# Transposes of 64 tokens on the two halves of the array, for groups 17 to 23 of an attention and mixture-of-depths kernel

## The chip, the cores and the metric

One core of one Trainium2 chip. The metric is the device time of one execution in microseconds (us), the median of several executions. Engines are named as in the profile: PE is TensorE's matrix multiply and PEld its weight load, DVE is VectorE, ACT is ScalarE, POOL is GpSimd, SP is SyncE, which only issues DMAs here.

## What is computed

The reference runs a linear attention with decay over blocks of 64 tokens (4 sequences, 8 heads, 768 tokens, 64 channels per head), and feeds its output to a mixture of depths: the 128 tokens of each sequence with the highest gate score go through two matrix products with a ReLU between them and are added back.

```
for b in range(nb):
    intra = (qb @ kb.T * Dmask) @ vb
    inter = (qb * lam_pow) @ kv_state
    out[:, :, sl] = intra + inter
    kv_state = lam_block * kv_state + (kb * rev_pow).T @ vb
...
scores = x @ w_gate
top_idx = argpartition(-scores[b], capacity)[:capacity]
ye = relu(x[b, top_idx] @ w1) @ w2
out[b, top_idx] = x[b, top_idx] + sigmoid(scores[b, top_idx])[:, None] * ye
```

All data is float32.

## The kernel before

The work goes in 24 groups of 128 tokens, six for each of the four sequences. A group's q, k and v lie in three tiles `qn`, `kn`, `vn` of 128 partitions (tokens) by 8 heads by 64 channels, loaded by SP some groups ahead. The order of the work is written out by hand: the last loop of the kernel goes over the groups, and each engine runs its instructions in that order. Groups 0 to 9 are "wide" and treat 128 tokens as one block; from group 10 on each group is two blocks of 64 tokens, and the array is used in quarters of 64 rows by 64 columns.

One iteration g of the loop (called round g) does, from group 10 on, in this order:

- `transposes(g + 1, ...)` (lines 217 to 232): four PE transposes of 128 by 128 for q (two heads each), four for k (L226), and after each four one ACT copy of 128 partitions by 512 out of PSUM (L230), to the tiles `qT` and `kT`.
- every sixth round (16 and 22 here) the gate of an expert step: four transposes of the fetched rows `xs` (L628) and an ACT copy to `xsT` (L633).
- `from_states(g)`: 16 products into the accumulator `o` (L381); `queries_decayed(g + 1)` on POOL, which multiplies `qT` to `qs` (L265); `state_products(g + 1)` into `su` (L327).
- one to three pieces of an expert's two matrix products (`hidden`, L657, with an ACT ReLU at L661; `back`, L669), between them a row of scores (L493) and sums over tables (L541) for the choice of tokens, which DVE does.
- `from_scores(g)`, 16 products into `o` (L403); `scores(g + 1)` into `su` (L285); `outputs(g)`: three ACT copies from `o` to the output tile `x_b`, one of 128 partitions (L433), two of 64 (L435), each between the halves of the partitions; `masked(g + 1)` on DVE, which makes `p` from `su` (L301).
- after a sequence's tokens have been chosen, `fetch` on POOL (L615) reads the chosen rows by an indirect DMA.

PSUM has two tiles `su` and `o` of two banks each and four banks handed out in turn by `bank()` (lines 186 to 195). A transposed group takes two of the four, and so do the row of scores, the sums and each expert product in turn one; whoever gets a bank again waits until the copy that reads it is done.

A matrix product of float32 shows as two records in the trace, a transpose as one. A form such as 64*128 behind a tile is the part of the array that is used: rows by columns.

Of the kernel before, what the change touches and what calls it, by code (L numbers as in the profile page):

```python
# [8 lines left out]
FP32 = mybir.dt.float32  # L9
# [8 lines left out]
def kernel(  # L18
# [12 lines left out]
    nc = tc.nc  # L31
# [5 lines left out]
    L = 128  # L37
    C = 64
    NT = S // L
    NHP = H // 2  # L40
# [3 lines left out]
    NG = B * NT  # L44
# [4 lines left out]
    W1 = (8, 8, 9, 10)  # L49
    W2 = (11, 11, 12, 13)  # L50
    WIDE = 10
    KEPT = {11: ((6, 2),), 12: ((8, 2), (10, 2))}
    KEPT.update((g + 4, ((g, 1),)) for g in range(12, 16))
    TINY = 2.0 ** -125
# [4 lines left out]
    att = ctx.enter_context(tc.tile_pool(name="att", bufs=3))  # L59
# [5 lines left out]
    half = [slice(0, C), slice(C, 2 * C)]  # L65
    loaded = {}
# [46 lines left out]
    ident = const.tile([128, 128], FP32, name="ident")  # L113
# [14 lines left out]
    for hp in range(NHP):  # L128
        for hh in range(2):
            h = 2 * hp + hh  # L130
            nc.vector.tensor_tensor_scan(
                out=mask_w[:, hh, hp, :], data0=lam_b[:, h : h + 1].broadcast_to([128, L]),
# [53 lines left out]
    def bank(hold=False):  # L186
        t = next(t for t in free if not any(t is x for x in held))
        free[:] = [x for x in free if x is not t] + [t]
        if hold:
            held.append(t)  # L190
        return t

    qTs, qss, kTs, kds, ps_ = {}, {}, {}, {}, {}
# [8 lines left out]
    def wide(g):  # L202
        return g < WIDE

    def keys_decayed(g):
        if g >= NG:
            return
        kd = att.tile([128, H, D], FP32, name="kd", bufs=2)
        pw = kpow_w if wide(g) else kpow
        nc.gpsimd.tensor_tensor(  # L210
            out=kd[:], in0=loaded[g][0][:],
            in1=pw[:].rearrange("p a b -> p (a b)").unsqueeze(2).broadcast_to([128, H, D]),
            op=ALU.mult,
        )
        kds[g] = kd

    def transposes(g, name):
        if g >= NG:
            return
        if wide(g - 1):  # L220
            tp = tq if name == "qT" else tk
        else:
            tp = bank()
        t = loaded[g][1 if name == "qT" else 0]
        for hp in range(NHP):
            nc.tensor.transpose(  # L226
                tp[:, hp * L : (hp + 1) * L], in_=t[:, 2 * hp : 2 * hp + 2, :], identity=ident[:]
            )
        dst = att.tile([128, NHP, L], FP32, name=name)
        nc.scalar.copy(out=dst[:].rearrange("p a i -> p (a i)"), in_=tp[:])  # L230
        (qTs if name == "qT" else kTs)[g] = dst

    def first_scores():
        got = []
# [201 lines left out]

    kept = {g + i for v in KEPT.values() for g, n in v for i in range(n)}

# [325 lines left out]
    def loads_to(n):  # L764
        while next_load[0] < min(n, NG):
            load(next_load[0])
            next_load[0] += 1

    def ends(g):
        return g >= 0 and g % NT == NT - 1  # L770

    def find(b):
        for i in range(NGR):
            hits(b, i)
# [6 lines left out]
    def shares(g):  # L781
        at = (g - WIDE) % NT
        if g + 1 == NG:
            return (0, 0, 1)
        few = at < 2 if g < WIDE + NT else at >= 4
        return (1, 0, 1) if few else (1, 1, 1)
# [57 lines left out]
    for g in range(-1, NG):  # L844
        loads_to(g + 4)
        for rows in KEPT.get(g, ()):
            rows_out(*rows)
        for do in weights.get(g, []):
            do()
        if wide(g):  # L850
            if g < 0:
                keys_decayed(0)
            wide_step(g)
            if g == 0:
                constants()
            if g == 1:
                narrow_constants()
        else:
            transposes(g + 1, "qT")
            transposes(g + 1, "kT")  # L860
            if NGR and ends(g - 5):
                for i in range(NGR):
                    gate, more = expert((g - 5) // NT, i)
                    if i == 0:
                        gate()
                    else:
                        pieces.append(gate)
                    pieces.extend(more)
            if g + 1 == NG:
                products(1)  # L870
            from_states(g)
            settle(g)
            queries_decayed(g + 1)
            state_products(g + 1)
            next_state(2 * g + 2)
            decay_state(2 * g + 3)
            keys_decayed(g + 2)
            share = shares(g)
            products(share[0])
            if NGR:  # L880
                column_sums(g - 2)
                row(g - 1)
            products(share[1])
            second(g + 1)
            if ends(g - 3):
                take((g - 3) // NT)
            if NGR:
                compare(g - 1)
                if ends(g - 2):
                    find((g - 2) // NT)  # L890
            products(share[2])
            from_scores(g)
            scores(g + 1)
            outputs(g)
            store(g)
            masked(g + 1)
            gate_scores(g)
            flush()
# [54 lines left out]
```

## Time and profile before

| | |
|---|---|
| median of 3 executions | 176.22 us (176.14 to 176.54) |
| the profiled execution's own time | 176.97 us |
| its span in the profile | 175.2 us |
| busy share of PE, PEld, DVE, ACT, POOL | 93%, 76%, 57%, 38%, 49% |
| granted TensorE clock, mean | 0.995 of full speed |

Times in the rows below are us from the start of the span. A row of the timeline gives the start, the time to the end of the last of its instructions, the engine, the line, what is written and read, and how many instructions were merged. A busy PE is one that has matmuls in flight, whose ends are modelled; the pace is read from starts. "idle before" in square brackets is the engine's idle time and what ended it.

### The profile page before, as it was taken

How to read it: one execution, taken by the hardware profiler on the slowest of the kernel's cores; microseconds unless marked ns; L12 is line 12 of the kernel's file. 1: busy time of each engine (PE TensorE's matmuls, PEld its weight loads, DVE VectorE, ACT ScalarE, POOL GpSimd, SP SyncE). 2: the span in 40 equal slices, each digit the busy share in tenths (PEclk: the TensorE clock that was granted, in tenths of full speed). 3: DMA queues.
4: the chain of work that ended last, by engine and by line, in shares of the span. 5: the costliest groups of instructions: out<-in, count | busy, mean ns of one | idle time of the engine just before them, and what ended most of it. 6: DMA issues, size and time to landing. Idle time of an engine off the chain costs nothing.

```text
span 175.2 us, 7559 instructions
## 1 busy us (share of the span) xinstructions
PE 162.9 (93%) x3250; PEld 132.4 (76%) x3250; DVE 99.9 (57%) x351; ACT 66.4 (38%) x170; POOL 86.1 (49%) x101
## 2 busy tenths in 40 slices
PE   6999999997999999998859999999999999999990
PEld 2778988886989898985444899975866999459970
DVE  3956567777766666567434545866656757530011
ACT  0552744443333456254031644542553545012100
POOL 2258966155489718745259264658468500202022
PEclk9999999999999999999999999999999999999998
DMA  4999999999999899999889997999893322011000
GB/s 108 227 219 225 236 209 237 232 237 223 208 239 269 188 253 223 283 277 308 239 200 229 200 259 177 228 191 244 190 191 112 123 62 62 8 55 60 0 30 30
DMA packets 92210, 31.94 MB, mean 182 GB/s; under 512 B 75793, under 2 KB 90129, under 8 KB 92178
## 3 DMA queue, kind: packets, MB, share of 16 engines
q1 hardware_dynamic: 91376, 29.37, 73.3%
q0 software_dynamic: 656, 2.10, 3.9%
q8 instruction: 25, 0.41, 1.0%
q14 instruction: 7, 0.06, 0.1%
q10 hardware_dynamic: 146, 0.01, 0.0%
HBM read 24.12 MB, written 7.34 MB: 180 GB/s over the span
## 4 chain that ended last, share of the span: by engine, by line
PE 59%; DMA 18%; SPq 8%; DVE 5%; issue 3%; ACT 2%; POOL 2%; POOLq 1%; ACTq 0%; DVEq 0%
DMA qn<-in_q_dram 11%; PE m L657 10%; PE m L226 9%; PE m L669 9%; DMA kn<-in_k_dram 6%; PE o L396 4%; PE su L279 4%; PE o L381 3%; PE su L327 3%; PE o L403 3%; PE su L285 3%; SPq L76 3%; PE o L370 3%; PE m L318 2%; PE m L696 2%
## 5 line engine op out<-in xcount | busy, mean ns | idle before, releaser
L657 PE MATMUL m<-xsT,w_sb 128*128 128x128 f32 x256 | 33.1, 280 | 0.0
L657 PEld LDWEIGHTS m<-xsT,w_sb 128*128 128x128 f32 x256 | 30.3, 192 | 1.4 <-ACT xsT L633 0.6
L265 POOL TENSOR_TENSOR qs<-qT,qpow 128x512 f32<-128x512 f32 x14 | 18.3, 1308 | 20.3 <-ACT qT L230 20.3
L669 PE MATMUL m<-w_sb,hs 128*128 128x512 f32 x48 | 24.0, 611 | 0.3 <-DMA w_sb<-in_moe_w_dram 0.3
L210 POOL TENSOR_TENSOR kd<-kn,kpow 128x512 f32<-128x512 f32 x14 | 15.1, 1078 | 6.3 <-DMA kn<-in_k_dram 6.3
L661 ACT ACTIVATE hs<-m 128x128 f32<-128x128 f32 x32 | 8.9, 277 | 24.0 <-PE m L657 19.1
L340 POOL TENSOR_TENSOR decayed<-state,decay 128x256 f32<-128x256 f32 x23 | 16.7, 726 | 2.2 <-DVE state L359 1.8
L226 PE MATMUL m<-ident,qn 128*128 128x128 f32 x92 | 14.7, 282 | 2.9 <-DMA qn<-in_q_dram 2.9
L263 POOL TENSOR_TENSOR qs<-qT,qpow 128x512 f32<-128x512 f32 x8 | 10.2, 1272 | 14.8 <-ACT qT L230 14.7
L301 DVE TENSOR_TENSOR p<-su,mask 128x512 f32<-128x512 f32 x14 | 9.7, 690 | 12.0 <-PE su L285 10.3
L230 ACT COPY qT<-m 128x512 f32<-128x512 f32 x23 | 13.4, 584 | 6.8 <-PE m L226 5.0
L295 DVE TENSOR_TENSOR p<-su,mask_w 128x1024 f32<-128x1024 f32 x10 | 12.2, 1220 | 6.5 <-PE su L279 6.5
L359 DVE TENSOR_TENSOR state<-su,decayed 128x256 f32<-128x256 f32 x23 | 9.8, 424 | 10.1 <-POOL decayed L340 5.7
L427 ACT COPY x_b<-o 128x512 f32<-128x512 f32 x10 | 5.9, 586 | 22.9 <-PE o L396 20.3
L226 PE MATMUL m<-ident,kn 128*128 128x128 f32 x92 | 13.8, 273 | 0.0
L230 ACT COPY kT<-m 128x512 f32<-128x512 f32 x23 | 13.6, 592 | 0.1
L226 PEld LDWEIGHTS m<-ident,qn 128*128 128x128 f32 x92 | 9.9, 141 | 4.8 <-DMA qn<-in_q_dram 3.5
L210 POOL TENSOR_TENSOR kd<-kn,kpow_w 128x512 f32<-128x512 f32 x10 | 10.4, 1045 | 4.9 <-DVE kpow_w L136 4.9
L403 PEld LDWEIGHTS o<-vn,p 64*64 64x64 f32 x448 | 7.8, 134 | 6.2 <-issue 1.5
L506 DVE TENSOR_SCALAR_CACHE_REDUCE table<-sc_row,sc 128x128 bf16<-128x128 f32 (+4 forms) x20 | 12.1, 604 | 0.0
L669 PEld LDWEIGHTS m<-w_sb,hs 128*128 128x128 f32 x48 | 8.0, 192 | 4.9 <-issue 4.1
L327 PE MATMUL su<-vn,kd 64*64 64x64 f32 x400 | 10.3, 221 | 1.4 <-issue 0.7
(103 smaller groups left out, 295.1 us busy)
## 6 DMA issues: line engine op xcount, KB each, us to landing
vn<-in_v_dram SPq DMA_DIRECT2D x24, 256.0 KB, 5.7
kn<-in_k_dram SPq DMA_DIRECT2D x23, 256.0 KB, 5.0
qn<-in_q_dram SPq DMA_DIRECT2D x23, 256.0 KB, 6.2
out_dram<-x_b SPq DMA_DIRECT2D x18, 256.0 KB, 4.6
w_sb<-in_moe_w_dram SPq DMA_DIRECT2D x16, 256.0 KB
out_dram<-x_b SPq DMA_DIRECT2D x3, 512.0 KB
kn<-in_k_dram SPq DMA_DIRECT2D x2, 128.0 KB
qn<-in_q_dram SPq DMA_DIRECT2D x2, 128.0 KB, 3.4
```

The source lines that it names most:

```text
L210: nc.gpsimd.tensor_tensor(out=kd[:], in0=loaded[g][0][:], in1=pw[:].rearrange("p a b -> p (a b)").unsqueeze(2).broadcast_to([128, H, D]), ...
L226: nc.tensor.transpose(tp[:, hp * L : (hp + 1) * L], in_=t[:, 2 * hp : 2 * hp + 2, :], identity=ident[:])
L230: nc.scalar.copy(out=dst[:].rearrange("p a i -> p (a i)"), in_=tp[:])
L263: nc.gpsimd.tensor_tensor(out=qs[:], in0=qTs[g][:], in1=qpow[:], op=ALU.mult)
L265: nc.gpsimd.tensor_tensor(out=qs[:].rearrange("p a (c i) -> p a c i", c=2), in0=qTs[g][:].rearrange("p a (c i) -> p a c i", c=2), in1=qpow ...
L295: nc.vector.tensor_tensor(out=p[:], in0=su[:], in1=mask_w[:].rearrange("p a b i -> p a (b i)"), op=ALU.mult,)
L327: nc.tensor.matmul(su[half[hh], c, NHP * C + hp * D : NHP * C + (hp + 1) * D], lhsT=kd[half[c], h, :], rhs=vn[half[c], h, :], start=True, ...
L340: nc.gpsimd.tensor_tensor(out=t[:], in0=states[n][:], in1=(decay_w if wide(g) else decay)[:], op=ALU.mult)
L403: nc.tensor.matmul(o_[half[hh ^ c], hh, hp * D : (hp + 1) * D], lhsT=p[half[c], hh, hp * C : (hp + 1) * C], rhs=vn[half[c], 2 * hp + hh, : ...
L506: nc.vector.tensor_scalar(out=table[:, : t * L], in0=rows_[b][:, : t * L], scalar1=scs[b][:, t : t + 1], scalar2=0.0, op0=ALU.is_ge, op1=A ...
L657: nc.tensor.matmul(ph, lhsT=w1_sb[:, dc, f * 128 : (f + 1) * 128], rhs=keep["xsT"][:, dc, :], start=(dc == 0), stop=(dc == NDC - 1),)
L669: nc.tensor.matmul(py[:], lhsT=keep["hs"][:, f, :], rhs=w2_sb[:, :, f, :], start=(f == 0), stop=(f == NFC - 1),)
```

## The change

For groups 17 to 23 (`SIDE = 17`, so in rounds 16 to 22) the eight transposes of 128 tokens are replaced by sixteen of 64 tokens. Tokens 0 to 63 lie in the upper half of the rows of the array and go to one PSUM bank, tokens 64 to 127 in the lower half and go to another; upper and lower alternate. A bank then holds one half of the tokens for q and, behind it, for k. The two ACT copies of 512 columns become four of 256, each of which writes four pieces of 64 columns with a stride. All sixteen transposes stand ahead of the four copies. Groups 0 to 16 keep the old form.

```diff
+    SIDE = 17
...
+    def side_by_side(g):
+        if g >= NG:
+            return
+        to = [bank(), bank()]
+        for i in range(2):
+            t = loaded[g][1 - i]
+            for hp in range(NHP):
+                for c in range(2):
+                    at = (i * NHP + hp) * C
+                    nc.tensor.transpose(
+                        to[c][:, at : at + C], in_=t[half[c], 2 * hp : 2 * hp + 2, :],
+                        identity=ident[half[c], half[c]],
+                    )
+        for i, (name, have) in enumerate((("qT", qTs), ("kT", kTs))):
+            dst = att.tile([128, NHP, L], FP32, name=name)
+            for c in range(2):
+                nc.scalar.copy(
+                    out=dst[:, :, half[c]],
+                    in_=to[c][:, i * NHP * C : (i + 1) * NHP * C].rearrange(
+                        "p (a i) -> p a i", i=C
+                    ),
+                )
+            have[g] = dst
...
-            transposes(g + 1, "qT")
-            transposes(g + 1, "kT")
+            if g + 1 >= SIDE:
+                side_by_side(g + 1)
+            else:
+                transposes(g + 1, "qT")
+                transposes(g + 1, "kT")
```

How the order on the engines moves, at three places. Behind `waits` stand the engines or DMA queues whose semaphores an instruction waits for; in the changed kernel the lines of the old functions are 27 higher (L381 is L408, L327 is L354, L493 is L520, L657 is L684, L633 is L660, L661 is L688). The first place is PE in round 18. Before:

```order
L226 MATMUL m_139<-ident,qn 128x128 [waits DMAHW7_49]
L226 MATMUL m_139<-ident,qn 128x128 x3
L226 MATMUL m_138<-ident,kn 128x128 [waits DMAHW6_49,DVE_49]
L226 MATMUL m_138<-ident,kn 128x128 x3
L381 MATMUL o<-state,qs 64x64 [waits Activation_49,Pool_49]
L381 MATMUL o<-state,qs 64x64 x7
L327 MATMUL su<-vn,kd 64x64 [waits DMAHW0_49,DVE_49,Pool_49]
```

Now, from the eight transposes of k on (the eight of q ahead of them look the same):

```order
L245 MATMUL m_139<-ident,kn 128x64 [waits DMAHW6_49]
L245 MATMUL m_138<-ident,kn 128x64
L245 MATMUL m_139<-ident,kn 128x64
L245 MATMUL m_138<-ident,kn 128x64
L245 MATMUL m_139<-ident,kn 128x64
L245 MATMUL m_138<-ident,kn 128x64
L245 MATMUL m_139<-ident,kn 128x64
L245 MATMUL m_138<-ident,kn 128x64
L408 MATMUL o<-state,qs 64x64 [waits Activation_49,Pool_49]
L408 MATMUL o<-state,qs 64x64 x7
L354 MATMUL su<-vn,kd 64x64 [waits DMAHW0_49,DVE_49,Pool_49]
```

The transposes have doubled in number and take turns between two banks; what follows, and what it waits for, is the same. L381's wait on Activation is for the last of the three output copies of the round before, L435.

The second place is ACT in round 16, whose expert gate stands behind the transposes. Before:

```order
L230 COPY qT_1869<-m0_138 128x512 [waits PE_49,Pool_49]
L230 COPY kT_1875<-m2_140 128x512 [waits DVE_49,PE_49,Activation_49]
L633 COPY xsT_1881<-m3_141 128x512 [waits PE_49]
L661 ACTIVATE hs_1883<-m1_139 128x128 [waits DVE_49,PE_49]
L497 COPY sc_row_1553<-m2_140 128x128 [waits PE_49]
```

Now:

```order
L252 COPY qT_1881<-m0_138 128x4x64 [waits PE_49,Pool_49]
L252 COPY qT_1881<-m2_140 128x4x64 [waits DVE_49,PE_49]
L252 COPY kT_1884<-m0_138 128x4x64 [waits Activation_49]
L252 COPY kT_1884<-m2_140 128x4x64
L660 COPY xsT_1891<-m3_141 128x512 [waits PE_49]
L688 ACTIVATE hs_1893<-m1_139 128x128 [waits DVE_49,PE_49]
```

The copy to `xsT`, which the first expert product reads, now has four copies ahead of it instead of two, and the first bank is read to the end by the third copy, the second by the fourth.

The third place is PE in round 17, where the row of scores and an expert product take the banks of the transposes again. Before:

```order
L541 MATMUL m1_139<-ones_146,table_1931 128x1
L493 MATMUL m0_138<-ident_99,sc_1472 128x128 [waits DVE_49,Activation_49]
L657 MATMUL m2_140<-xsT_1881,w1_sb_97 128x128 [waits Activation_49]
L657 MATMUL m2_140<-xsT_1881,w1_sb_97 128x128 x3
L657 MATMUL m3_141<-xsT_1881,w1_sb_97 128x128 [waits Activation_49]
```

Now:

```order
L568 MATMUL m1_139<-ones_146,table_1941 128x1
L520 MATMUL m0_138<-ident_99,sc_1472 128x128 [waits DVE_49,Activation_49]
L684 MATMUL m2_140<-xsT_1891,w1_sb_97 128x128 [waits Activation_49]
L684 MATMUL m2_140<-xsT_1891,w1_sb_97 128x128 x3
L684 MATMUL m3_141<-xsT_1891,w1_sb_97 128x128 [waits Activation_49]
```

The order is the same, but L493's bank was free after the copy of qT and is now free after the third copy, and the bank of the L657 behind it was free after the copy of kT and is now free after the fourth.

## Rows read from the trace of the kernel before

**Rows 1.** The page: busy time by engine, and shares of the chain that ended last.

```profile
PE 162.9 (93%) x3250; PEld 132.4 (76%) x3250; DVE 99.9 (57%) x351; ACT 66.4 (38%) x170; POOL 86.1 (49%) x101
...
PE 59%; DMA 18%; SPq 8%; DVE 5%; issue 3%; ACT 2%; POOL 2%; POOLq 1%; ACTq 0%; DVEq 0%
```

**Rows 2.** The chain that ended last, in order of time: start, duration, what.

```profile
83.83 6.77 DMA qn<-in_q_dram
...
90.64 1.09 PE m L226 x8
...
111.08 1.02 PE m L226 x8
...
141.80 0.69 DVE p L301
```

**Rows 3.** Timeline of PE and ACT in round 18.

```profile
109.92 0.69 PE L403 MATMUL o<-vn,p 64*64 64x64 f32 x32
...
110.44 0.65 PE L285 MATMUL su<-qT,kT 64*64 64x64 f32 x32
...
110.68 0.37 ACT L433 COPY x_b<-o 128x256 f32<-128x256 f32 x1 [0.38 <-PE o L403]
...
111.02 0.66 PE L226 MATMUL m<-ident,qn 128*128 128x128 f32 x4
111.07 0.74 ACT L435 COPY x_b<-o 64x256 f32<-64x256 f32 x2
...
111.51 0.60 PE L226 MATMUL m<-ident,kn 128*128 128x128 f32 x4
111.84 0.58 ACT L230 COPY qT<-m 128x512 f32<-128x512 f32 x1
...
112.04 0.51 PE L381 MATMUL o<-state,qs 64*64 64x64 f32 x10
...
112.32 0.59 ACT L230 COPY kT<-m 128x512 f32<-128x512 f32 x1
```

**Rows 4.** Timeline of PE in a wide round: products on the two halves.

```profile
24.37 1.16 PE L279 MATMUL su<-qT,kT 64*128 64x128 f32 x16
25.46 1.15 PE L396 MATMUL o<-vn,p 128*64 128x64 f32 x32
```

**Rows 5.** Timeline of PE in rounds 16 and 17: expert products behind the transposes.

```profile
100.39 1.16 PE L657 MATMUL m<-xsT,w_sb 128*128 128x128 f32 x8
...
107.73 0.30 PE L493 MATMUL m<-ident,sc 128*128 128x128 f32 x1
107.94 0.49 PE L657 MATMUL m<-xsT,w_sb 128*128 128x128 f32 x2
```

**Rows 6.** Timeline of ACT in rounds 16 and 17.

```profile
98.66 0.59 ACT L230 COPY qT<-m 128x512 f32<-128x512 f32 x1
99.14 0.59 ACT L230 COPY kT<-m 128x512 f32<-128x512 f32 x1
99.62 0.60 ACT L633 COPY xsT<-m 128x512 f32<-128x512 f32 x1
...
106.83 0.57 ACT L230 COPY qT<-m 128x512 f32<-128x512 f32 x1
107.30 0.59 ACT L230 COPY kT<-m 128x512 f32<-128x512 f32 x1
```

**Rows 7.** Timeline of POOL, DVE and PE in rounds 20 and 21.

```profile
125.03 1.27 POOL L265 TENSOR_TENSOR qs<-qT,qpow 128x512 f32<-128x512 f32 x1 [2.50 <-ACT qT L230]
...
128.94 1.00 POOL L615 DMA_INDIRECT xs<-out_dram,tok  x1 [0.16 <-issue]
...
130.35 0.69 DVE L301 TENSOR_TENSOR p<-su,mask 128x512 f32<-128x512 f32 x1 [1.70 <-PE m L226]
...
131.15 0.69 PE L327 MATMUL su<-vn,kd 64*64 64x64 f32 x32 [0.33 <-issue]
```

**Rows 8.** Timeline of ACT at the start, two windows: copies of 128 x 256.

```profile
6.27 0.70 ACT L245 COPY first<-m 128x256 f32<-128x256 f32 x2
...
6.27 0.97 ACT L245 COPY first<-m 128x256 f32<-128x256 f32 x3
```

## The prediction

> **What bounds the kernel now.** I read the page first: TensorE (PE) is busy 93% of the span, and PE work is 59% of the chain that ended last [rows 1]. That share is an average, so I read the chain in order of time. There the last wait for a load ends at 90.64 us; from then on the chain is PE work alone, eight transposes of 1.02 us in each round among them, until 141.80, where VectorE (DVE) takes over [rows 2]. The seven rounds that the change touches (call the iteration g of the main loop "round g"; it transposes group g + 1, so rounds 16 to 22) lie in that stretch. So PE time taken out would count in full, if nothing else is waiting right behind it. That has to be read round by round from the timeline.
>
> Round 18 shows it [rows 3]. The transposes start at 111.02 and the next PE work, L381, at 112.04. But L381 accumulates into tile o, and o is still being read: the three output copies of ScalarE (ACT, L433 and L435) start at 110.68, after L403, and end at 111.07 + 0.74 = 111.81. The order of the program says that L381 waits for the last of them (Activation among its waits). So PE has only 111.81 to 112.04 = 0.23 us less a hand-over to gain there, however fast the transposes become. What I see: two paths of nearly equal length from L403 to L381, one of them on ACT and untouched by the change.
>
> **The transposes themselves.** Eight records with 128 columns moved become sixteen with 64 columns, alternating between the halves of the array. Nearest rows: L279 uses the same halves (64*128), loads 128 columns per record and moves 128: 16 records from 24.37 to 25.46, 1.09 us, 68 ns each, two at a time [rows 4]. L285 moves 64 columns with four quarters of the array at a time: 32 records from 110.44 to 111.02, 0.58 us, 18 ns each, so about 73 ns per quarter [rows 3]; two at a time that is 36 ns, or 0.58 us for sixteen. Bounds 0.58 and 1.09 us against 1.02 now. I take 0.58, because the columns moved set the pace in both rows and here they are 64. Sixteen loads instead of eight are hidden behind the other half's records, as they are in L279; if that cover is gone, see the slow rival.
>
> The Trainium skill (TensorE: Matmul & The Clock Gate, section LDWEIGHTS) says that a load's time goes by its columns, not by its rows: P/1.2 ns, and that 32 x 128 takes as long as 128 x 128. By it sixteen loads in a row would take 1.71 us (an estimate) and the halves would lose. L279's 68 ns per record with the same 128 columns shows that loads of two halves do overlap or are quicker, so I give that little chance.
>
> **What the saved 0.44 us buys in each round.**
> - Rounds 18 and 19: L381 starts when the output copies have ended plus a hand-over. In round 17 PE starts hidden product L657 at 107.94, 0.05 us after the copy of kT out of the same bank ended (107.30 + 0.59 = 107.89) [rows 5, 6]; L381 has two waits, so I take 0.10. Gain 0.23 - 0.10 = 0.13 each; ends 0 and 0.18. Everything behind L381 is PE work in order, so it is kept. Sum -0.26.
> - Round 20 would gain the same, but gives it to round 21. There the fetch of the expert rows starts on GpSimd (POOL) at 128.94; p (L301) on DVE, though its scores were done before, starts only at 130.35, and L327, which writes the same tile, at 131.15 [rows 7]. POOL works without a gap from qs at 125.03 to that fetch, and qs waits for the two new halves of qT. So what counts for rounds 20 and 21 is when qT is complete: see ACT.
>
> **ACT: two copies of 512 columns become four of 256.** One of 512 takes 0.58 to 0.59 us and starts 0.48 after the one before (98.66, 99.14, 99.62) [rows 6]; one of 256 takes 0.37 (L433) [rows 3]. How close behind each other can the short ones start? Two ends: the output copies do not overlap at all (110.68, 111.07, then 0.74 for two: 0.37 to 0.39 apart) [rows 3]; the copies of 256 columns at the very start do: two end at 6.97, three at 7.24, 0.27 apart [rows 8]. I take 0.27: like the new ones and like qT to kT, those run over all 128 partitions from partition 0, while the output copies shift between the halves of the partitions. Four copies then take 1.06 to the next start instead of 0.96.
> - Round 16: ACT starts qT at 98.66, xsT would start at 99.72 instead of 99.62 and end at 100.33; L657 needs it, at 100.38 with the hand-over, and it starts at 100.39 now [rows 5, 6]. PE comes there 0.44 early and waits: 0.0. The same in round 22, which has the same expert gate: 0.0.
> - Round 17: ACT is held by the gate's exponential until 106.83, whatever PE does. The fourth copy ends at 106.83 + 3 x 0.27 + 0.37 = 108.01; the hidden product writes the same bank and starts at 108.06 instead of 107.94 [rows 5, 6]: +0.11. The 0.13 at L381 is lost in that wait.
> - Rounds 20 and 21: qT is complete 0.27 + 0.37 = 0.64 after its start instead of 0.59: +0.05.
>
> DMA: nothing is issued more or less, no queue is passed. POOL, DVE: no instruction changes.
>
> **Sum.** 0.0 + 0.11 - 0.13 - 0.13 + 0.05 + 0.0 = -0.10 us. The profiled execution took 176.97 us (span 175.2 and 1.77 around it), 0.75 above the median of 176.22; I carry the difference over to the median: 176.1. A measurement of this kernel can tell about 0.2%, 0.35 us, from no change, so this is no change.
>
> **Rivals.**
> - The ACT copies do not overlap (0.375 apart, as the output copies). Round 16: xsT starts at 98.66 + 1.50, L657 at 100.82: +0.42; round 22 the same; round 17: 108.38, +0.44; rounds 18 and 19 -0.26; rounds 20 and 21 +0.16. Sum +1.18: 177.4, slower. If only copies into the same tile fail to overlap, +0.7: 176.9. It decides from about 0.30 us between copies on. For it: the new copies write strided rows of 4 x 64, as L433 does. Against: rows 8 and the overlap of qT and kT. Chance 0.25.
> - The halves do not run side by side as fast. At L279's 1.09 us the copies, which wait for all sixteen records, start 0.49 late: rounds 16 and 22 +0.47 each, 17 +0.11, 18 and 19 +0.07 each, 20 and 21 +0.54: +1.7, 178.0; chance 0.07. If each half record cost as much as a whole one now (16 x 0.128 = 2.04 us), every round would lose 1.0 and rounds 16, 20 and 22 1.4: +7, 183.5; chance 0.04. L279 speaks against that.
> - ACT is better still: copies 0.21 apart, the pure difference of 0.58 and 0.37 for 256 columns. Then xsT comes 0.2 earlier in rounds 16 and 22, round 17 gains 0.05, rounds 18 and 19 up to 0.18 each: -0.8, 175.4, faster. Rows 8 show no pair so close, but there PE's transposes may have held it. Chance 0.15.
>
> **Numbers.** Forecast 0.49. It spreads by the hand-over (rounds 18 and 19: 0 to -0.36 in all) over 175.9 to 176.4; a tenth of it may pass 0.35 on the fast side. Faster: 0.15 + 0.05 = 0.20. Slower: 0.25 + 0.11 = 0.36, of which a little may stay within: 0.35. Same: 0.45. The range takes in the copies without overlap and the fast ACT: 175.4 to 177.6; outside lie the slow halves (0.11) and a tail.
>
> **What would show it.** Right: sixteen records in about 0.6 us; L381 0.1 us after the last output copy with PE idle 0.3 before it; copies of 256 columns 0.27 apart; L657 waiting for xsT in rounds 16 and 22. Wrong: copies 0.37 apart; 1 us or more for the sixteen records; or L381 starting before the output copies end.

## The result and the profile after

The changed kernel takes 178.04 us (median of 12 executions, 176.75 to 180.70) where the kernel before took 175.87 beside it: a ratio of 1.0122, 95% interval 1.0080 to 1.0164. That is 2.2 us slower, not the same. Timed twice more (e2 and e9 below), it came to 1.0017 (0.9977 to 1.0057) and 1.0144 (1.0067 to 1.0222); two of the three intervals lie above 1, so the sign is fairly safe, the size is not.

The profiled execution took 177.48 us, span 175.7. The page: busy time of PE, the queue that carries an engine's instructions (queue, packets, MB, share of the DMA engines), and the shares of the last chain, to be laid beside [rows 1].

```profile
PE 160.3 (91%) x3306; PEld 130.0 (74%) x3306; DVE 100.4 (57%) x351; ACT 67.1 (38%) x184; POOL 85.8 (49%) x101
...
q8 instruction: 26, 0.43, 1.0%
...
PE 40%; POOL 14%; DMA 13%; issue 11%; SPq 7%; DVE 7%; ACT 5%; POOLq 1%; DVEq 0%; ACTq 0%
```

PE is busy 2.6 us less than before and the kernel is longer: "issue", time in which an engine waits for nothing that the profile shows, has gone from 3% to 11% of the chain. That share has to be read by place. Of its 20 us some 15 lie ahead of 46 us, where both kernels do the same work, and e2, the same kernel, has 3%. In the seven changed rounds the two longest pieces of it are these:

```profile
128.87 0.53 issue
...
134.28 0.60 issue
```

Groups of PE work by line, with the idle time ahead of them and what ended it, first in the kernel before, then after:

```profile
L381 PE MATMUL o<-state,qs 64*64 64x64 f32 x416 | 10.0, 224 | 0.2 <-issue 0.2
L285 PE MATMUL su<-qT,kT 64*64 64x64 f32 x448 | 9.1, 218 | 0.2 <-DVE state L359 0.2
```

```profile
L312 PE MATMUL su<-qT,kT 64*64 64x64 f32 x448 | 10.1, 219 | 1.6 <-issue 1.4 <-DVE state L386 0.2
L408 PE MATMUL o<-state,qs 64*64 64x64 f32 x416 | 9.9, 225 | 0.9 <-ACT x_b L462 0.9
```

L408's new 0.9 us is the wait for the output copies that the prediction described. L312's 1.4 us is not in the prediction at all. The steps that it did describe came as described. PE and ACT in round 16:

```profile
97.63 0.46 PE L245 MATMUL m<-ident,qn 64*128 64x64 f32 x8
...
98.27 0.65 PE L655 MATMUL m<-ident,xs 128*128 128x128 f32 x4
...
100.19 0.49 PE L684 MATMUL m<-xsT,w_sb 128*128 128x128 f32 x2 [0.18 <-ACT xsT L660]
```

```profile
98.45 0.65 ACT L252 COPY qT<-m 128x256 f32<-128x256 f32 x2
98.98 0.67 ACT L252 COPY kT<-m 128x256 f32<-128x256 f32 x2
99.51 0.63 ACT L660 COPY xsT<-m 128x512 f32<-128x512 f32 x1
```

The sixteen records take 97.63 to 98.27 = 0.64 us, and a pair of copies starts 0.53 after the pair before, 0.27 a copy. Round 18, beside [rows 3]:

```profile
110.94 0.47 PE L245 MATMUL m<-ident,qn 64*128 64x64 f32 x8
110.99 0.74 ACT L462 COPY x_b<-o 64x256 f32<-64x256 f32 x2
...
111.88 0.51 PE L408 MATMUL o<-state,qs 64*64 64x64 f32 x10 [0.23 <-ACT x_b L462]
```

The copies end at 110.99 + 0.74 = 111.73 and L408 follows 0.15 later. The stretches from one round's transposes to the next one's, the last to the end, show where the time went:

| round | 16 | 17 | 18 | 19 | 20 | 21 | 22 to the end | sum |
|---|---|---|---|---|---|---|---|---|
| before, us | 6.71 | 6.47 | 6.27 | 6.25 | 5.47 | 5.94 | 40.23 | 77.34 |
| after, us | 6.72 | 6.59 | 6.21 | 6.18 | 6.32 | 5.84 | 40.20 | 78.06 |

From round 16 on the kernel is 0.72 us longer, and round 20 alone 0.85. PE there and in round 21:

```profile
128.22 0.65 PE L312 MATMUL su<-qT,kT 64*64 64x64 f32 x29
129.39 0.33 PE L312 MATMUL su<-qT,kT 64*64 64x64 f32 x3 [0.53 <-issue]
...
133.99 0.30 PE L312 MATMUL su<-qT,kT 64*64 64x64 f32 x6
134.89 0.68 PE L312 MATMUL su<-qT,kT 64*64 64x64 f32 x26 [0.60 <-issue]
```

PE stops in the middle of the scores, after 29 of 32 records and after 6 of 32, for 0.74 and 0.82 us from one start to the next, with no tile to wait for. Before, the same scores run through in both rounds:

```profile
128.43 0.65 PE L285 MATMUL su<-qT,kT 64*64 64x64 f32 x32
...
134.37 0.65 PE L285 MATMUL su<-qT,kT 64*64 64x64 f32 x32
```

Round 21 is not longer than before only because L327 waits for a late p there [rows 7], which it does not after.

**The theory.** I counted PE's instructions in the program, a product and its weight load as one each: 6582 before, 6687 after, sixteen more in each of the seven changed rounds (and seven separate waits fewer). The two gaps stand after instruction 5570 and after instruction 5826, exactly 256 apart. The packets of q8 are 16 KB each, 25 before and 26 after, which is one per 256 instructions. The packet that belongs to the first gap starts at 127.03 and PE goes on 2.36 us later; for the second it is 132.60 and 2.29 us. So: PE's instructions come in stretches of 256, one packet each, and where PE works off a stretch before the next one has come, it stands. Halved transposes give it more instructions in less time. Against this stand waits on tiles, and plain scatter between executions. In what follows a boundary is the place between two stretches, and a stretch is entered when its first product starts.

The Trainium skill (Runtime: NRT & Kernel Launch, section Instruction fetch mechanics) says that an engine's sequencer fetches its program in blocks of 256 instructions by a DMA queue of its own while it runs the block before, and that crossing such a boundary is mostly hidden. The trace agrees with the first half (one 16 KB packet per 256 instructions) and not with the second (0.74 and 0.82 us at two boundaries). I had not set that section against the change.

### The profile page after: what moved, and what is told of

The parts are those of the page before. It is cut to its first block, busy times and chain, and to the rows that moved or that the text cites. A ratio compares the mean times of both kernels' runs of the same rounds, so it can differ in the third digit from the quotient of the medians.

```text
span 175.7 us, 7677 instructions
## 1 busy us (share of the span) xinstructions
PE 160.3 (91%) x3306; PEld 130.0 (74%) x3306; DVE 100.4 (57%) x351; ACT 67.1 (38%) x184; POOL 85.8 (49%) x101
## 4 chain that ended last, share of the span: by engine, by line
PE 40%; POOL 14%; DMA 13%; issue 11%; SPq 7%; DVE 7%; ACT 5%; POOLq 1%; DVEq 0%; ACTq 0%
PE m L684 13%; PE m L696 9%; DMA kn<-in_k_dram 6%; POOL kd L211 5%; POOL qs L290 5%; DMA qn<-in_q_dram 4%; PE o L430 3%; PE o L408 3%; PE su L312 3%; POOL decayed L367 3%; SPq L77 2%; SPq L101 2%; PE su L354 2%; PE m L723 2%; PE m L227 2%
## 5 line engine op out<-in xcount | busy, mean ns | idle before, releaser
L684 PE MATMUL m<-xsT,w_sb 128*128 128x128 f32 x256 | 33.1, 280 | 0.4 <-ACT xsT L660 0.3
L684 PEld LDWEIGHTS m<-xsT,w_sb 128*128 128x128 f32 x256 | 30.3, 192 | 2.0 <-ACT xsT L660 1.2
L292 POOL TENSOR_TENSOR qs<-qT,qpow 128x512 f32<-128x512 f32 x14 | 17.8, 1271 | 20.0 <-ACT qT L252 12.0
L367 POOL TENSOR_TENSOR decayed<-state,decay 128x256 f32<-128x256 f32 x23 | 17.6, 765 | 1.7 <-DVE state L386 1.5
L211 POOL TENSOR_TENSOR kd<-kn,kpow 128x512 f32<-128x512 f32 x14 | 14.6, 1041 | 7.2 <-DMA kn<-in_k_dram 7.2
L688 ACT ACTIVATE hs<-m 128x128 f32<-128x128 f32 x32 | 8.9, 278 | 23.4 <-PE m L684 19.1
L290 POOL TENSOR_TENSOR qs<-qT,qpow 128x512 f32<-128x512 f32 x8 | 10.2, 1273 | 15.4 <-ACT qT L231 15.3
L227 PE MATMUL m<-ident,qn 128*128 128x128 f32 x64 | 10.2, 281 | 4.2 <-DMA qn<-in_q_dram 4.2
L231 ACT COPY qT<-m 128x512 f32<-128x512 f32 x16 | 9.4, 584 | 7.8 <-PE m L227 6.5
L312 PE MATMUL su<-qT,kT 64*64 64x64 f32 x448 | 10.1, 219 | 1.6 <-issue 1.4
L423 PE MATMUL o<-vn,p 128*64 128x64 f32 x320 | 11.5, 225 | 0.0
L460 ACT COPY x_b<-o 128x256 f32<-128x256 f32 x14 | 5.2, 372 | 15.8 <-PE o L430 14.3
L227 PEld LDWEIGHTS m<-ident,qn 128*128 128x128 f32 x64 | 6.9, 141 | 5.7 <-DMA qn<-in_q_dram 4.2
```

Source lines behind the costliest of these rows:

```text
L211: nc.gpsimd.tensor_tensor(out=kd[:], in0=loaded[g][0][:], in1=pw[:].rearrange("p a b -> p (a b)").unsqueeze(2).broadcast_to([128, H, D]), ...
L227: nc.tensor.transpose(tp[:, hp * L : (hp + 1) * L], in_=t[:, 2 * hp : 2 * hp + 2, :], identity=ident[:])
L290: nc.gpsimd.tensor_tensor(out=qs[:], in0=qTs[g][:], in1=qpow[:], op=ALU.mult)
L292: nc.gpsimd.tensor_tensor(out=qs[:].rearrange("p a (c i) -> p a c i", c=2), in0=qTs[g][:].rearrange("p a (c i) -> p a c i", c=2), in1=qpow ...
L312: nc.tensor.matmul(su[half[c], hh, hp * C : (hp + 1) * C], lhsT=kT[half[hh], hp, half[c]], rhs=qT[half[hh], hp, half[c]], start=True, stop ...
L367: nc.gpsimd.tensor_tensor(out=t[:], in0=states[n][:], in1=(decay_w if wide(g) else decay)[:], op=ALU.mult)
```

## The experiments

The part ahead of round 16 is the same work in both kernels, but its start of round 16 lay anywhere from 95.56 to 99.71 us in the traces that follow. So I compare the stretch from the transposes of round 16 to the end ("the late part") between traces, and the ratio of the timed executions beside it. From round 16 to round 22 the granted clock is 1.00 of full speed in every trace, so the clock has no part in these differences.

| run | late part, us | ratio to before (95%) |
|---|---|---|
| e1 before again | 77.38 | 0.9987 (0.9953 to 1.0022) |
| e2, e9 after again | 78.14, 78.77 | 1.0017, 1.0144 (see above) |
| e3 after, shift 48 | 78.15 | 0.9978 (0.9937 to 1.0019) |
| e4 after, shift 112 | 78.81 | 1.0045 (1.0008 to 1.0081) |
| e5, e10 after, late stores | 76.97, 77.36 | 1.0068 (1.0032 to 1.0105), 1.0045 (0.9995 to 1.0096) |
| e6, e11 before, late stores | 76.80, 76.69 | 0.9983 (0.9942 to 1.0023), 1.0055 (1.0010 to 1.0099) |
| e7 before, shift 128 | 77.36 | 1.0003 (0.9968 to 1.0039) |
| e8 after, copy on VectorE | 80.34 | 1.0200 (1.0146 to 1.0254) |
| e12 after, late stores, products moved | 79.54 | 1.0178 (1.0104 to 1.0251) |
| e13, e18 the same, rounds 17 to 21 only | 77.73, 77.89 | 0.9957 (0.9925 to 0.9989), 0.9987 (0.9937 to 1.0036) |
| e14, e15 after, before without last loads | 78.57, 77.31 | 1.0012 (0.9971 to 1.0052), 1.0009 (0.9972 to 1.0047) |
| e16 after without the gather | 76.76 | not timed (one execution) |
| e17 e13 with shift 48 | 77.09 | 1.0017 (0.9979 to 1.0056) |

### Do the gaps stay with the instruction count? (e1 to e4, e7, e9)

e1, e2 and e9 are the two kernels unchanged. e3, e4 and e7 put dummy products into round 15, 24 or 56 in the kernel after, 64 in the kernel before:

```diff
+    def pad(n):
+        t = next(t for t in free if not any(t is x for x in held))
+        for _ in range(n):
+            nc.tensor.matmul(
+                t[:, 0:1], lhsT=pad_w[:], rhs=ones[:], start=True, stop=True
+            )
...
+            if g == 15:
+                pad(24)
```

> The kernel before, unchanged, beside the others on one chip. All theories: the ratio to the kernel before is 1.000 within 0.3%. The theory (PE runs out of instructions): its PE has gaps that end on no wait inside a line at most in one place of the last loop, about 0.3 to 0.4 us, since the stretches of 256 PE instructions in rounds 16 to 22 take 4 us or more each. Rival (the difference between the two kernels is only that between runs): the median of this kernel scatters by as much as the kernel after differs, 2 us.

> The kernel after, unchanged. The theory (in rounds 20 and 21 PE reaches the end of a fetched stretch of 256 instructions before the next has come): 1.0 to 1.5% slower than the kernel before again, and the gaps that end on no wait stand in the scores L312 of round 20 after 29 of its 32 records and of round 21 after 6 of its 32, 0.5 to 0.9 us each, at the same instructions as in the trace shown. Rival (waits on tiles, such as L408 on the last output copy): slower by as much, but with the gaps in other places from run to run. Rival (runs scatter): within 0.3% of the kernel before.

> The kernel after with 24 dummy products (48 PE instructions) in round 15, where PE waits for qn for 1.5 us or more; their results are overwritten. Every boundary of 256 PE instructions behind them moves 48 instructions forward in the work. The theory: the shortest stretch of 256 is then 3.85 us (at 108.3 us) where it was near 3.4 us, and the stalls of rounds 20 and 21 shrink from 1.35 us together to 0.5 us or less: 176.5 to 177.2 where the kernel after gives 178.0. Rival (waits on tiles, or scatter): the same time as the kernel after within 0.3 us, or longer by the time of the dummies if they show (24 x 55 ns = 1.3 us).

> The kernel after with 56 dummy products (112 PE instructions) in round 15; their results are overwritten. The boundaries move 112 instructions. The theory: the boundaries now fall so that two stretches of 256 take 2.5 us (ending at 127.4 us) and 2.7 us (at 103.0 us); PE stalls at both for 1 to 2 us, and the time is 1 to 2 us longer than that of the kernel after, 179 to 180. Rival (waits on tiles, or scatter): the same as the kernel after, plus at most what the dummies take beyond PE's wait for qn (56 x 55 ns = 3.1 us against 1.5 us of wait: up to 1.6 us, all of it seen before L245 of round 16, with no gap inside L312 or L327 of the later rounds).

> The kernel before with 64 dummy products (128 PE instructions) in round 15, their results overwritten: no transpose is halved, only the boundaries of 256 PE instructions move by 128. The theory: the shortest stretch is then one of 2.9 us that ends near 106.5 us (round 17, in the outputs or scores of round 17 to 18), and PE has a gap there of 0.5 to 1.2 us that no wait ends; from the transposes of round 16 to the end 77.9 to 78.5 us, against 77.34 and 77.38. Rival (stalls belong to the halved transposes): no new gap, 77.4.

> The kernel after, unchanged, a third time, beside the next three. The theory (the whole loss is PE's wait for its instructions in rounds 20 and 21): 78.0 to 78.2 us from the transposes of round 16 to the end, and 0.3 to 0.6% slower than the kernel before in the timed runs. Rival (the halved transposes cost something besides, ahead of round 16 or in another way): the timed difference is again 1.0 to 1.5% where the trace from round 16 on shows 0.4%.

Timeline of PE in e2:

```profile
129.50 0.65 PE L312 MATMUL su<-qT,kT 64*64 64x64 f32 x29
130.30 0.33 PE L312 MATMUL su<-qT,kT 64*64 64x64 f32 x3 [0.16 <-issue]
...
135.44 0.30 PE L312 MATMUL su<-qT,kT 64*64 64x64 f32 x6
136.32 0.67 PE L312 MATMUL su<-qT,kT 64*64 64x64 f32 x26 [0.59 <-issue]
```

The same records, 29 and 3, 6 and 26. In e9 the second gap is longer:

```profile
132.11 0.30 PE L312 MATMUL su<-qT,kT 64*64 64x64 f32 x6
133.62 0.68 PE L312 MATMUL su<-qT,kT 64*64 64x64 f32 x26 [1.21 <-issue]
```

With the boundaries moved by 112 instructions (e4) L312 is whole, and L354 is cut in rounds 17 and 21:

```profile
105.46 0.55 PE L354 MATMUL su<-vn,kd 64*64 64x64 f32 x20
106.66 0.45 PE L354 MATMUL su<-vn,kd 64*64 64x64 f32 x12 [0.65 <-issue]
...
131.23 0.56 PE L354 MATMUL su<-vn,kd 64*64 64x64 f32 x20 [0.26 <-issue]
132.31 0.45 PE L354 MATMUL su<-vn,kd 64*64 64x64 f32 x12 [0.52 <-issue]
```

And the kernel before, moved by 128 (e7), has a gap of its own in round 17, after 27 of the 32 records of L327:

```profile
106.90 0.63 PE L327 MATMUL su<-vn,kd 64*64 64x64 f32 x27
107.99 0.33 PE L327 MATMUL su<-vn,kd 64*64 64x64 f32 x5 [0.47 <-issue]
```

The kernel before unchanged has one too, ahead of the changed rounds; in e1 it cuts L285 after 28 of 32 records, where the trace of before shows none:

```profile
67.28 0.68 PE L285 MATMUL su<-qT,kT 64*64 64x64 f32 x28 [0.22 <-DVE state L359]
68.20 0.33 PE L285 MATMUL su<-qT,kT 64*64 64x64 f32 x4 [0.24 <-issue]
```

The longest stands in e2, also ahead of the change:

```profile
82.92 0.65 PE L354 MATMUL su<-vn,kd 64*64 64x64 f32 x30
86.18 0.28 PE L354 MATMUL su<-vn,kd 64*64 64x64 f32 x2 [2.61 <-issue]
```

Each of these gaps stands at the instruction count of a boundary, and no halved transpose is needed for one. That is shown. The gaps end 2.2 to 2.9 us after the start of their packet in every run. Sizes were missed: e2 is 0.2% slower than before, not 1.0 to 1.5; e4 is 0.7 us behind after in the late part, not 1 to 2; e9 is 1.4% slower, not 0.3 to 0.6, with a late part of 78.77. The shift by 48 did take the gaps of rounds 20 and 21 down (0.11 us at the one boundary, none at the other), but two new ones of 0.41 and 0.42 us came in rounds 17 and 18, and in round 21 p was late as in the kernel before (DVE idle 1.65 us ahead of it; the round took 5.70 us where e16 takes 5.21), so the late part did not shrink (78.15). And e7's late part stayed at 77.36, because its gap in round 17 (7.08 us instead of 6.47) was paid back in round 21 (5.29 instead of 5.94), of which more below.

### What makes the packet late? (e5, e6, e10, e11, e14 to e16)

Late stores, for both kernels:

```diff
     KEPT.update((g + 4, ((g, 1),)) for g in range(12, 16))
+    KEPT[22] = ((18, 3),)
```

> The kernel after, but with the output rows of groups 18, 19 and 20 (3 x 256 KB) issued on SP at the head of round 22 in place of the ends of rounds 18 to 20: the same PE instructions, less on the DMA engines between 118 and 132 us. The theory (a stretch of 256 PE instructions comes by a DMA packet that waits behind the loads and stores, and PE stalls when it comes later than about 2.3 us after that packet's start): the packets of rounds 20 and 21 start 1 to 2 us after the stretch before was entered, where it was 2.6 and 3.2 us, the two gaps in L312 shrink from 1.35 us together to 0.4 us or less, and the stretch from the transposes of round 16 to the end takes 77.0 to 77.3 us where it took 78.06 and 78.14. Rival (the gaps are PE's own, at these instructions, whatever the DMA does): 1.35 us of gaps again, 78.1. Rival (the time is lost to the waits on output copies at L408): 78.1, with no change in any round.

> The kernel before with the same three stores issued at the head of round 22: the control for the run above. The theory: before has no such gap in these rounds, so from the transposes of round 16 to the end it takes 77.1 to 77.4 us, as without the move (77.34 and 77.38). Rival (later stores help in another way, by the loads landing sooner): it gains as much as the kernel after does, 0.5 us or more.

> The kernel after with the stores of groups 18 to 20 at the head of round 22, again. The theory: 76.9 to 77.1 us from round 16 to the end, and 0.5 to 0.8% faster than the kernel after of the same call. Rival (something else costs 1 us or more in the kernels with halved transposes, as the 1.2 us by which this kernel was slower than the kernel before in its first timing): again 0.5% or more slower than the kernel before.

> The kernel before with the same late stores, again: 76.7 to 76.9 us from round 16 to the end where the kernel before took 77.34 and 77.38, and 0.2 to 0.4% faster than it in the timed runs. If the 0.55 us are not seen in the timed runs, the part ahead of round 16 scatters by more than they are.

Timeline of PE in e5:

```profile
128.53 0.65 PE L313 MATMUL su<-qT,kT 64*64 64x64 f32 x32
...
133.74 0.30 PE L313 MATMUL su<-qT,kT 64*64 64x64 f32 x6
134.19 0.68 PE L313 MATMUL su<-qT,kT 64*64 64x64 f32 x26 [0.16 <-issue]
```

The first gap is gone and the second is 0.38 us from start to start; the late part is 1.1 us shorter than after's, as expected (77.36 in e10, with 0.70 left at the second gap and round 20 0.3 longer than in e5). But the second packet still started 3.04 and 3.19 us after the stretch before was entered, not 1 to 2. And the control moved too: the kernel before gained 0.55 to 0.7 us, all of it in round 21. The timed ratios follow none of this: e5 and e11 are 0.7 and 0.55% slower than before, with late parts 0.4 and 0.65 us shorter. So there are differences of 1.5 us and more that the late part does not hold. In e11 no transpose is halved, so they do not need the change; what makes them is open.

Without the last loads:

```diff
     def load(g):
+        if g > 20:
+            loaded[g] = loaded[20]
+            return
```

> The kernel after, but groups 21 to 23 are not loaded (9 loads of 256 KB from round 17 on are left out; these groups compute on group 20's rows, so the output of groups 21 to 23 is not the reference's). The instructions of PE are the same. The theory (the instruction packets wait behind loads and stores): from about 120 us on the packets start 1 us or less after the stretch before was entered, there is no gap at a boundary in rounds 19 to 21, round 20 takes 5.4 and round 21 5.3 us, and it is 76.4 to 76.7 us from round 16 to the end. Rival (packets are late whatever the DMA engines do): gaps of 0.4 to 1.4 us at L312 in rounds 20 and 21 again, 77.8 to 78.8.

> The kernel before with the same loads left out (output of groups 21 to 23 not the reference's). The theory: round 21 takes 5.3 us as with late stores, 76.6 to 76.8 us from round 16 to the end; against the run of the kernel after with the same loads left out, the halved transposes are then worth what the prediction gave them, 0.0 to 0.4 us. Rival (the halved transposes lose by something else than instruction supply): the kernel before is 0.5 us or more ahead here too.

Timeline of PE in e14, and the packets of all queues from 130.75 to 132.25 us:

```profile
130.30 0.65 PE L315 MATMUL su<-qT,kT 64*64 64x64 f32 x32
...
136.25 0.30 PE L315 MATMUL su<-qT,kT 64*64 64x64 f32 x6
137.05 0.68 PE L315 MATMUL su<-qT,kT 64*64 64x64 f32 x26 [0.50 <-issue]
```

```profile
DMA packets 0, 0.00 MB, mean 0 GB/s; under 512 B 0, under 2 KB 0, under 8 KB 0
```

Here the simple form of my theory fell. The first gap went, as expected, but the second stayed (0.72 us from start to start, late part 78.57 and not 76.4 to 76.7), and its packet started at 134.78, 4.06 us after the stretch before was entered at 130.72, although not one packet of any queue ran for the first 1.5 us and more of that. It is not the amount of traffic. What did stand ahead of it was the gather of the chosen rows: GpSimd prepares it from 130.84 on (L645 there), its packets and those of a store then run, and the instruction packet starts as they end. Taking the gather away:

```diff
     def fetch(b, i):
+        if b == 2:
+            xss[b, i] = xss[1, i]
+            return
```

> The kernel after without the gather of batch 2's rows on GpSimd in round 20 (the experts of batch 2 compute on batch 1's rows, so their output is not the reference's). PE's instructions are the same. If the packet for the second gap waits behind the gather: it starts 1.0 to 1.7 us after the stretch before was entered (3.2 to 3.7 us in the kernel after), the gap in L312 of round 21 (0.8 to 1.4 us) is gone, and round 21 takes 5.3 us. The gap in L312 of round 20 (0.4 to 0.7 us), whose packet starts before the gather, stays. Rival (the packet's moment hangs on PE's own work): the gap of round 21 stays at 0.7 us or more.

Timeline of PE in e16:

```profile
126.63 0.65 PE L312 MATMUL su<-qT,kT 64*64 64x64 f32 x32
...
131.84 0.65 PE L312 MATMUL su<-qT,kT 64*64 64x64 f32 x32
```

In e16 the packet starts 1.64 us after the stretch before was entered (3.21 in after), the gap of round 21 is gone, and the round takes 5.21 us. So the gather delays that packet: one execution without it shows this, and the other traces agree. Where the stretch before was entered 0.18 us or more ahead of the gather (e3, e4, e7, e12, e17), the packet starts 1.1 to 2.1 us after entry, ahead of the gather's first packet. Where it was entered from 0.12 us before to 0.67 us after the gather began (after, e2, e5, e8, e9, e10, e13, e14, e18), it starts 2.5 to 4.1 us after entry and 2.9 to 4.0 us after the gather began, when most of the gather's packets have run. The first gap went too, which I had not expected; its packet started 0.97 us after entry where it was 2.56, 2.17 and 2.20 in the three traces of the kernel after. That one went in e5 and e14 as well, so it hangs on something that all three lighten; what, is open. In e15, the control for e14, round 21 kept its 5.94 us where 5.3 was expected.

### The wait at L408 (e8, e12, e13, e17, e18)

In the kernel after four rounds (17 to 20) hold 0.23 us each at L408, in e5 and e16 round 21 as well. Two ways to use them: the last output copy on VectorE, or expert products moved into the wait (with late stores).

```diff
-        for c in range(2):
-            nc.scalar.copy(out=x_b[half[c], t, :, 1, :], in_=po[1][half[1 - c]])
+        nc.scalar.copy(out=x_b[half[0], t, :, 1, :], in_=po[1][half[1]])
+        (nc.vector.tensor_copy if 16 <= g else nc.scalar.copy)(
+            out=x_b[half[1], t, :, 1, :], in_=po[1][half[0]]
+        )
```

```diff
+            share = shares(g)
             if g + 1 == NG:
                 products(1)
+            elif 17 <= g <= 21:
+                products(share[0])
             from_states(g)
...
-            share = shares(g)
-            products(share[0])
+            if not 17 <= g <= 21:
+                products(share[0])
```

> The kernel after, with the last of the three output copies of a group (64 partitions x 256) on VectorE in place of ScalarE from group 16 on, so that the bank that L408 waits for is free some 0.3 us sooner. If the copies on ScalarE hold L408 as predicted, the wait of 0.23 us before L408 goes in rounds 17 to 21 and each of these rounds would be 0.2 to 0.3 us shorter, 1.0 to 1.5 us in all. The theory (PE's instruction supply bounds these rounds): less than half of that arrives, 77.3 to 78.0 from round 16 to the end against 78.06 and 78.14, and the gaps at the boundaries of 256 instructions grow. Rival (waits on tiles bound them): all of it arrives, 76.6 to 77.1.

> The kernel after with the late stores, and from round 16 on the first piece of an expert's products (8 products L684 or 2 of L696, about 1 us) moved ahead of L408, into the 0.23 us that PE waits there for the output copies. If that wait is all that keeps the halved transposes from their gain: 0.2 us less in each of rounds 17 to 21, 76.0 to 76.4 us from round 16 to the end, against 76.97 without the move, and faster than the kernel before by 0.5% or more. Rival (the states, which come a microsecond later, then hold the outputs L430 or the decays on GpSimd hold the products): no gain or a loss, 76.9 to 78. The theory adds that rounds of 5.2 us leave PE's instructions less time: a gap at a boundary of 256 instructions in rounds 20 or 21.

> The kernel after with the late stores and with the first piece of products moved ahead of L408 in rounds 17 to 21 alone (rounds 16 and 22, where the moved products had to wait 1.3 us for xsT, are as in the kernel after). By the run before: rounds 17, 18 and 19 take 6.46, 6.01 and 6.06 us where they took 6.59, 6.20 and 6.17; with rounds 16 and 22 at 6.7 and 40.25, from the transposes of round 16 to the end 76.2 to 76.9 us, the spread being what is left of the gaps at boundaries in rounds 20 and 21 (0 to 0.7). Rival (the wait at L408 only moves): 77.0 to 77.4 as in the two runs with late stores.

> The version with late stores and moved products (rounds 17 to 21), and 24 dummy products (48 PE instructions) in round 15, their results overwritten: the boundary that cost 1.33 us in L312 of round 20 moves by 48 instructions. By the stretches of that version's trace the gaps shrink from 1.3 us to 0.3 to 0.8 us: 76.6 to 77.1 us from round 16 to the end (77.73 without the shift), and 0.4 to 0.9% faster than the kernel before in the timed runs if the dummies stay in PE's wait for qn in round 15. Rival (the boundary is not what cost it): 77.7 again.

> The version with late stores and moved products (rounds 17 to 21) again: 77.0 to 77.8 us from round 16 to the end with a gap of 0.7 to 1.4 us in L312 of round 20, and within 0.4% of the kernel before or faster. The kernel before takes 77.3 to 77.4, so a clear gain in the timed runs would have to come from ahead of round 16, where the two are the same but for scatter.

e8 made it worse, a late part of 80.34 us. The copy on VectorE does not run beside the one on ScalarE: in the program it waits for a semaphore of ScalarE's copy of the other half. So it follows it, takes 0.42 us where ScalarE's takes 0.37, and L408 waits longer (0.31 us). The run therefore does not test what it was made for. A timeline of DVE and one of PE:

```profile
110.96 0.42 DVE L462 COPY x_b<-o 64x256 f32<-64x256 f32 x1 [0.47 <-ACT x_b L461]
```

```profile
111.52 0.68 PE L408 MATMUL o<-state,qs 64*64 64x64 f32 x16 [0.31 <-DVE x_b L462]
```

e12 (products moved from round 16 on) lost 1.3 us each in rounds 16 and 22, where the moved products need xsT:

```profile
98.84 0.82 PE L685 MATMUL m<-xsT,w_sb 128*128 128x128 f32 x5 [1.27 <-ACT xsT L661]
```

e13 leaves those two alone. In round 18 L409 now follows the products without a wait, and the gap has gone to round 20:

```profile
111.71 1.16 PE L685 MATMUL m<-xsT,w_sb 128*128 128x128 f32 x8
112.80 0.39 PE L409 MATMUL o<-state,qs 64*64 64x64 f32 x6
...
127.79 0.68 PE L313 MATMUL su<-qT,kT 64*64 64x64 f32 x29
129.58 0.33 PE L313 MATMUL su<-qT,kT 64*64 64x64 f32 x3 [1.11 <-issue]
```

Rounds 18 and 19 take 6.01 and 5.97 us, 0.2 less each than in e5. But the boundary in round 20 costs 1.33 us, in e18 again 1.33, which is more than all that the move gains; the late parts, 77.73 and 77.89, miss the 76.2 to 76.9 and 77.0 to 77.8 that were expected. A shift by 48 (e17) cut that gap to 0.45 and the late part to 77.09, but the 0.4 to 0.9% expected of it did not come. None of it is safely faster than the kernel before: e13's interval lies below 1 (0.9957), that of the same kernel in e18 does not (0.9987), nor does e17's (1.0017).

## Why the prediction was wrong

**The step that failed** is the cost of more instructions. The prediction said of sixteen loads in place of eight that they "are hidden behind the other half's records", which holds inside the array, and "DMA: nothing is issued more or less, no queue is passed". Both leave out that the instructions themselves have to come, by packets on a DMA queue: a cost that was put at nothing without a reason. In its place the traces show gaps at boundaries, 0.74 and 0.82 us in after, 0.38 and 0.81 in e2, 0.44, 0.38 and 1.43 in e9, and the late part longer by 0.7 to 1.4 us.

**Where the 2.2 us are.** 0.7 to 1.4 us are located, in the traces of the late part. In the trace of after the two gaps cost 1.5 us; 0.7 is left of it, since round 21 of before loses 0.65 to its late p. The rest of the 2.2 us is not located. The work ahead of round 16 is the same in both kernels, and in the traces it is not longer in the kernel after (round 16 begins at 97.63, 99.01 and 95.72; before at 97.84 and 98.18). The two executions that were traced differ by 0.5 us only (177.48 and 176.97), so the traces hold all of their own difference, and the other 1.7 us lie between executions of which there is no trace. What makes them is open.

**Point by point, the rest held, but for rounds 20 and 21.**
- Transposes: 0.58 us predicted, 0.64 measured, 0.04 us a record. So both rivals with slow halves (1.09 us, and 2.04 us at the cost of whole records) are out. By the Trainium skill's rule on weight loads (TensorE: Matmul & The Clock Gate, section LDWEIGHTS), sixteen loads in a row would take 1.71 us, by the prediction's estimate; the 0.64 us do not agree with loads in a row, so the loads of the two halves overlap here.
- L408 behind the output copies: right in place. The hand-over was 0.15, not 0.10, so rounds 18 and 19 gained 0.06 and 0.07, not 0.13 each.
- Copies 0.27 apart: right, so the likeliest rival (0.375 apart, +1.18) is out, and so is the one with a faster ACT. That the measured time came near the rivals with 177.4 and 178.0 us is chance; their causes are absent. (The rival with 183.5 us is added up wrongly: four rounds at 1.0 and three at 1.4 make 8.2, not 7. It had a chance of 0.04, and nothing else hangs on it.)
- Rounds 16 and 22: 0.0 predicted, +0.01 and -0.03 measured. Round 17: +0.11 predicted, +0.12 measured.
- Rounds 20 and 21: +0.05 predicted, +0.75 measured. Its reasoning was wrong as well: it read before's L327 in round 21 as the end of a chain from qs over the gather to p [rows 7]. In e6 and e7 the same gather stands in the same place of POOL's order and p is not late; round 21 takes 5.29 us there against 5.94. With the loads left out (e15) it takes 5.94 again. The trace's semaphore events tell what p waits for. The last record of the scores L285 ends at 129.07 (a modelled end), and PE's semaphore, for which p and the next copy of qT wait, rises only at 130.33, 1.26 us later and 1.39 after the gather began. So the scores were done, and the word of it was late. In e1, e15, e2, e3, e4 and e14 it is 0.8 to 1.3 us late in the same place, in e5, e6, e7 and e11 0.14 us, and in e16, without the gather, 0.06. What decides between the two is open.

**What the change is worth where instructions come in time:** after without gaps (e16) takes 36.28 us from round 16 to the start of round 22, before without its late p (e11) 36.47: 0.19 faster, from two traces of which one leaves out the gather. The sum had said 0.10. The sum over the tiles was near in total, though not in each round, and what bound the kernel was not a tile.

## What to carry to other kernels

Splitting a product into more and smaller ones costs instructions even where the array hides it: count the instructions of the engine per microsecond. In rounds 16 to 22 here all six stretches of 256 that PE worked off in under 3.6 us ended in a stall that no tile explains; those of 3.9 to 5.7 us did so only where the packet started 1.5 us or more after the stretch before it was entered (at the gaps it is 2.2 to 2.9 us from packet to use). Look for idle time marked "issue" that cuts a run of equal records at the same record in every execution; a few dummy products ahead of it, in an idle place, show whether it moves with the count. A share of the chain, such as issue, says nothing until its pieces are read in order of time. And where the start of a kernel scatters, compare traces from a point behind it.

## What the hardware showed that I had not expected

- PE stands for want of instructions for 0.4 to 1.4 us at boundaries of 256 instructions in the late part, once for 2.8 us ahead of it (e2), in code without a branch.
- The packet starts from 1.1 us before to 4.1 us after the stretch before it is entered, the latest with idle DMA engines for 1.5 us of that time (e14); a gather that GpSimd has begun goes ahead of it (3.21 us with the gather, 1.64 without; e16, and the order in the other traces).
- While a gather of GpSimd had just begun, PE's semaphore rose 0.8 to 1.3 us after the last record of the scores in seven traces, and 0.14 us after it or less in the others.
